# A linear-attention and SwiGLU kernel: batch 0 without arithmetic on GpSimd, a new order on VectorE and PE, and a weight load exchanged with a batch load

## The chip, the cores and the metric

The kernel runs on one core of a Trainium2 chip. The metric is the device time in microseconds (us), taken as the median of several executions. The record marks every execution told of here as fast, so that none has to be set aside. The profile's span is about 2 us shorter than the device time, because it starts with the first instruction. A time such as "at 21.2 us" counts from the start of that span. The engines are PE (TensorE, matrix products), VectorE (DVE in the profile), ScalarE (ACT), GpSimd (POOL) and SyncE (SP).

## The reference

```python
def _attn_ref(q, k, v):                  # 8 batches, 8 heads, 576 tokens, head size 64
    def phi(x):
        return np.where(x > 0, x, np.exp(x) - 1.0) + 1.0
    q_p, k_p = (phi(q), phi(k))
    kv = np.einsum('bhsd,bhse->bhde', k_p, v)
    z = np.sum(k_p, axis=2)
    num = np.einsum('bhsd,bhde->bhse', q_p, kv)
    den = np.einsum('bhsd,bhd->bhs', q_p, z)[..., None] + 1e-06
    return (num / den).astype(np.float32)

def _moe_ref(x, w_gate, w_val, w_out):   # 4608 tokens, 512 -> 1536 -> 512
    g = x @ w_gate
    silu = g * (1.0 / (1.0 + np.exp(-g)))
    return (silu * (x @ w_val) @ w_out).astype(np.float32)
```

The attention's output, with heads side by side, is the x of the feed-forward.

## The kernel before

The tokens are worked off in nine groups of 512. Each group passes through L1 (twelve blocks `fb` of the hidden size, gate and value) and then L2 (`wo`). These two stages keep PE full. Batches 0 and 1 are special. Batch 0 must pass through the whole attention before the first L1 matmul can start: this is the *prologue*. Batch 1 is worked off beside the first L1 and L2.

For batch 0 the feature map is built from two terms, since phi(x) = max(x, 0) + min(exp(x), 1). A head group `lp` (0 or 1) holds half of the heads. Before the change, GpSimd computed three of the instructions of lp 1:

```python
def k_max(lp):
    term(k16[0], kp[1], lp, 0.0, ALU.max, (nc.vector, nc.gpsimd)[lp])
def k_sum(lp):
    c = slice(P * lp, P * lp + P)
    (nc.vector, nc.gpsimd)[lp].tensor_tensor(out=kp[0][:, :, c], in0=kp[0][:, :, c], in1=kp[1][:, :, c], op=ALU.add)
def q_max(b, lp):
    term(q16[b], qp[1], lp, 0.0, ALU.max, (nc.vector, nc.gpsimd)[lp])
```

GpSimd also issues all loads, in program order. So its arithmetic stands between them:

```python
# ... loads of batch 0 and of w1's columns 0:256
q_max(0, 1)          # GpSimd
k_max(1)             # GpSimd
ld_w1(256, 512)
# ... VectorE, ScalarE and PE work of batch 0
k_sum(1)             # GpSimd
ld_w1(512, 768); ld_k(1); ld_w1(768, 1024); ld_w1(1024, 1280); ld_q(1); ld_w1(1280, 1536)
ld_w2(0); ld_v(1); ld_k(2); ld_w2(1); ld_w2(2)
```

`ld_w2(i)` loads a third of `wo`. In the first L2 stage, work of batches 1 and 2 is put into twelve slots, one after each four matmuls. The stage goes three times through the four output tiles (`i` = 0, 1, 2):

```python
w = at(12, [ # ... slots 0 to 2: transposes, z and k-v products of batch 1
    (2, lambda: exp_k(2, 0)), (2, lambda: exp_k(2, 1)), (3, lambda: den1(0)), (3, lambda: phi_k(2, 0)),
    (4, lambda: num1(0)), (5, lambda: den1(1)), (5, lambda: phi_k(2, 1)), (6, lambda: num1(1)),
    (7, lambda: den2()), (8, lambda: num2()), (9, lambda: exp_q(2, 0)), (10, lambda: exp_q(2, 1))])
# ...
for i in range(3):
    for t in range(4):
        l2(0, t, 4 * i, 4 * i + 4)
        for f in w[4 * i + t]:
            f()
        if i == 2:
            l2_out(0, t, V)      # VectorE copies the finished tile out of PSUM
vcast(2, 0)
```

`exp_k` runs on ScalarE and `phi_k` (one minimum, then two combined maximum-and-add instructions) on VectorE. `den1`, `den2` take PE, then ScalarE (ln, then exp); `num1`, `num2` take PE, then VectorE. The four output tiles lie in the PSUM banks (where PE puts its results) pV[0], pG[0], pV[1], pG[1]. The next L1 stage writes pG[0] and pV[0] first.

## Time and profile before

| what | before |
|---|---|
| device time, median of the four runs beside the changed kernel | 331.31 us (330.93 to 331.93) |
| first L1 matmul | 21.21 us |
| block 2 of L1 (the first one not mixed with the prologue) | 27.91 us |
| first L2 matmul | 45.53 us |
| second L1 stage begins | 61.76 us |
| from there to the end of the span | 267.6 us |

The table of stretches of the kernel before shows where PE has room. The columns are the stretch in us, its length, the busy time of each engine with its count of instructions, the granted PE clock (1.00 is full speed), the DMA share and GB/s.

```profile
8.00:16.00 8.00, 4.74 (x81) 3.51 (x78) 6.55 (x7) 5.81 (x7) 6.23 (x2) 1.00 1.19 185
16.00:20.00 4.00, 1.75 (x44) 1.07 (x44) 3.62 (x9) 1.17 (x2) 3.99 (x4) 0.83 0.74 91
20.00:28.00 8.00, 7.86 (x59) 3.35 (x60) 2.27 (x6) 2.24 (x6) 7.45 (x11) 0.66 1.10 146
28.00:44.00 16.00, 16.00 (x75) 7.27 (x75) 11.98 (x24) 15.22 (x17) 6.13 (x9) 1.00 1.33 200
```

From 28 us on PE is full at full clock, and only work that lets it start sooner can save time. Between 8 and 20 us PE is busy for about half of the time. Between 16 and 28 us the clock is also reduced. The trace's clock record gives 0.50 from 18.65 to 25.48 us.

The wait list of PE of the kernel before (who waited for whom: us in total, times, longest) names GpSimd three times:

```profile
PE pG_112 L393 <- POOL kp_72 L365: 1.3, 1, 1.3
PE pV_116 L165 <- POOL kp_71 L377: 1.3, 1, 1.3
...
PE pV_114 L405 <- POOL qp_74 L365: 1.0, 1, 1.0
```

Now the timeline of GpSimd and after it that of VectorE, before (start, duration, engine, line, operation, tiles, shape):

```profile
9.77 3.12 POOL L365 TENSOR_SCALAR qp_74<-q_0_65 128x1152 f16<-128x1152 f16 x1 [2.28 <-DMA q_0_65<-in_q_dram]
12.89 3.29 POOL L365 TENSOR_SCALAR kp_72<-k_0_63 128x1152 f16<-128x1152 f16 x1
...
17.69 2.39 POOL L377 TENSOR_TENSOR kp_71<-kp_71,kp_72 128x1152 f16<-128x1152 f16 x1
```

```profile
6.58 0.46 DVE L365 TENSOR_SCALAR kp_71<-ek 128x1152 f16<-128x1152 f16 x1 [0.74 <-ACT ek L362]
...
10.99 2.21 DVE L365 TENSOR_SCALAR qp_73<-eq 128x1152 f16<-128x1152 f16 x1
13.13 3.36 DVE L365 TENSOR_SCALAR kp_71<-ek 128x1152 f16<-128x1152 f16 x1
```

An instruction of the same form takes VectorE 0.46 us at 6.58 us, when GpSimd does no arithmetic. Beside GpSimd's instructions it takes 2.21 and 3.36 us. Each ends 0.31 us after GpSimd's instruction beside it: 13.20 after 12.89, and 16.49 after 16.18. In these two lines a busy VectorE is therefore mostly a blocked VectorE. The Trainium skill, "SBUF — State Buffer", section "Who interferes with whom", describes a port pair that the two engines share and that one of them holds for a whole instruction; these two pairs fit it.

The end of the first L2 stage, before: the first two output copies on VectorE, then PE's first matmul of the next stage.

```profile
60.13 0.68 DVE L306 TENSOR_SCALAR osb_102<-pV_114 128x512 f32<-128x512 f32 x1
60.73 0.68 DVE L306 TENSOR_SCALAR osb_103<-pG_112 128x512 f32<-128x512 f32 x1
```

```profile
61.76 0.38 PE L275 MATMUL pG_112<-xT_1_91,wg 128*128 128x512 f16 x1
```

The copy out of pG frees the bank at 61.4 us, and PE finishes L2 only then. Nothing waits.

### The profile page before, as it was taken

How to read it: one execution, taken by the hardware profiler on the slowest of the kernel's cores; microseconds unless marked ns; L12 is line 12 of the kernel's file. 1: busy time of each engine (PE TensorE's matmuls, PEld its weight loads, DVE VectorE, ACT ScalarE, POOL GpSimd, SP SyncE). 2: the span in 40 equal slices, each digit the busy share in tenths (PEclk: the TensorE clock that was granted, in tenths of full speed). 3: DMA queues.
4: the chain of work that ended last, by engine and by line, in shares of the span. 5: the costliest groups of instructions: out<-in, count | busy, mean ns of one | idle time of the engine just before them, and what ended most of it. 6: DMA issues, size and time to landing. Idle time of an engine off the chain costs nothing.

```text
span 329.4 us, 5083 instructions
## 1 busy us (share of the span) xinstructions
PE 317.2 (96%) x1957; PEld 150.0 (46%) x1957; DVE 220.0 (67%) x398; ACT 167.6 (51%) x239; POOL 40.5 (12%) x50
## 2 busy tenths in 40 slices
PE   8579999999999999999999999999999999999994
PEld 6434454454444444544444444444444444444443
DVE  3855776688978885888588858885887344234321
ACT  3626998927844684458445844584431233123310
POOL 7895410010001000100010000000000000000000
PEclk9969999999999999999999999999999999999999
DMA  7999999999395538363737340224112410140014
GB/s 106 175 125 177 203 207 208 218 225 152 65 159 105 105 80 166 57 115 75 148 71 125 63 100 15 26 54 97 27 24 48 98 32 0 31 91 8 2 32 96
DMA packets 40984, 32.18 MB, mean 98 GB/s; under 512 B 16256, under 2 KB 36480, under 8 KB 40960
## 3 DMA queue, kind: packets, MB, share of 16 engines
q0 software_dynamic: 20640, 18.88, 37.1%
q1 hardware_dynamic: 20160, 12.85, 17.8%
q8 instruction: 15, 0.25, 0.3%
q10 hardware_dynamic: 160, 0.13, 0.2%
q14 instruction: 9, 0.07, 0.1%
HBM read 37.75 MB, written 9.44 MB: 143 GB/s over the span
## 4 chain that ended last, share of the span: by engine, by line
PE 82%; ACT 5%; DVE 5%; issue 3%; DMA 2%; POOL 1%; SPq 0%; ACTq 0%; POOLq 0%; DVEq 0%
PE pG_112 L275 13%; PE pG_113 L275 12%; PE pV_114 L275 8%; PE pV_115 L275 8%; PE pV_116 L275 8%; PE pV_115 L296 7%; PE pG_112 L296 7%; PE pV_114 L296 7%; PE pG_113 L296 6%; DMA q_0_65<-in_q_dram 2%; PE pX_118 L165 2%; DVE hT_98 L281 1%; DVE kp_71 L365 1%; ACT ek L121 1%; ACT sil_100 L280 1%
## 5 line engine op out<-in xcount | busy, mean ns | idle before, releaser
L275 PEld LDWEIGHTS <-wv 128*128 128x128 f16 x432 | 42.5, 98 | 51.6 <-issue 1.1
L275 PEld LDWEIGHTS <-wg 128*128 128x128 f16 x432 | 41.4, 98 | 50.7 <-issue 2.1
L280 ACT ACTIVATE sil_100<-pG_112 128x512 f16<-128x512 f32 x51 | 30.5, 597 | 51.7 <-PE pG_112 L275 45.6
L280 ACT ACTIVATE sil_101<-pG_113 128x512 f16<-128x512 f32 x51 | 30.5, 597 | 37.8 <-PE pG_113 L275 35.1
L296 PEld LDWEIGHTS <-hT_98 128*128 128x128 f16 x228 | 21.4, 98 | 26.0 <-issue 1.5
L296 PEld LDWEIGHTS <-hT_99 128*128 128x128 f16 x192 | 18.4, 98 | 22.8 <-issue 0.9
L306 DVE TENSOR_SCALAR osb_104<-pV_115 128x512 f32<-128x512 f32 x9 | 6.2, 689 | 16.8 <-PE pV_115 L296 16.8
L215 DVE TENSOR_REDUCE den<-prod 128x12 f32<-128x768 f16 x18 | 17.0, 943 | 0.0
L296 PE MATMUL pV_114<-wo,hT_98 128*128 128x512 f16 x60 | 14.1, 379 | 0.2 <-DVE hT_98 L281 0.2
L296 PE MATMUL pV_115<-wo,hT_98 128*128 128x512 f16 x60 | 14.1, 379 | 0.0
L296 PE MATMUL pG_112<-wo,hT_98 128*128 128x512 f16 x60 | 14.1, 379 | 0.0
L281 DVE SCALAR_TENSOR_TENSOR hT_98<-pV_114,sil_100 128x512 f16<-128x512 f32 x11 | 7.6, 691 | 8.4 <-PE pV_114 L275 6.3
L304 ACT ACTIVATE osb_103<-pG_112 128x512 f32<-128x512 f32 x8 | 4.7, 584 | 16.3 <-PE pG_112 L296 16.3
L306 DVE TENSOR_SCALAR osb_105<-pG_113 128x512 f32<-128x512 f32 x8 | 5.5, 691 | 9.4 <-PE pG_113 L296 9.4
L296 PE MATMUL pG_113<-wo,hT_98 128*128 128x512 f16 x48 | 11.4, 380 | 0.0
L296 PE MATMUL pG_113<-wo,hT_99 128*128 128x512 f16 x48 | 11.1, 380 | 0.0
L296 PE MATMUL pV_114<-wo,hT_99 128*128 128x512 f16 x48 | 11.0, 379 | 0.0
L296 PE MATMUL pG_112<-wo,hT_99 128*128 128x512 f16 x48 | 11.0, 379 | 0.0
L296 PE MATMUL pV_115<-wo,hT_99 128*128 128x512 f16 x48 | 11.0, 379 | 0.0
L275 PE MATMUL pG_113<-xT_0_90,wg 128*128 128x512 f16 x27 | 10.5, 388 | 0.0
L275 PE MATMUL pG_113<-xT_0_92,wg 128*128 128x512 f16 x27 | 10.5, 388 | 0.0
L275 PE MATMUL pG_112<-xT_0_90,wg 128*128 128x512 f16 x27 | 10.5, 388 | 0.0
(240 smaller groups left out, 745.2 us busy)
## 6 DMA issues: line engine op xcount, KB each, us to landing
k_1_64<-in_k_dram POOLq DMA_DIRECT2D x4, 576.0 KB, 7.3
q_1_66<-in_q_dram POOLq DMA_DIRECT2D x4, 576.0 KB, 9.4
v_1_68<-in_v_dram POOLq DMA_DIRECT2D x4, 576.0 KB, 11.5
out_dram<-osb_102 SPq DMA_DIRECT2D x18, 128.0 KB, 2.4
out_dram<-osb_103 SPq DMA_DIRECT2D x18, 128.0 KB, 2.4
out_dram<-osb_104 SPq DMA_DIRECT2D x18, 128.0 KB, 2.4
out_dram<-osb_105 SPq DMA_DIRECT2D x16, 128.0 KB, 2.6
k_0_63<-in_k_dram POOLq DMA_DIRECT2D x3, 576.0 KB, 15.8
```

What stands on the lines that cost most here:

```text
L121: nc.scalar.activation(out=e[:, s, :], in_=src[b % 2][:, s, :], func=AF.Exp, bias=0.0, scale=1.0)
L165: nc.tensor.matmul(out=kvb[b][hh][:, 256 * lp:256 * lp + W], lhsT=kp[b % 2][rows, j, P * lp:P * lp + P], rhs=vv, start=(j == 0), stop=(j = ...
L215: nc.vector.tensor_reduce(out=den[:, HL * j0:HL * j1], in_=prod[:, 0:j1 - j0, :].rearrange("p j (l d) -> p (j l) d", d=D), axis=AX.X, op=A ...
L275: nc.tensor.matmul(out=ps[:, :], lhsT=src[:, i, P * fb:P * fb + P], rhs=xT[i][g % 2][:, :], start=(i == 0), stop=(i == 3))
L280: nc.scalar.activation(out=s[:, :], in_=pg[:, :], func=AF.Silu, bias=0.0, scale=1.0)
L281: nc.vector.scalar_tensor_tensor(out=hT[g % 2][:, fb, :], in0=pv[:, :], scalar=SC, in1=s[:, :], op0=ALU.mult, op1=ALU.mult)
L296: nc.tensor.matmul(out=pso[(g, t)][:, :], lhsT=hT[g % 2][:, fb, P * t:P * t + P], rhs=wo[:, fb, :], start=(fb == 0), stop=(fb == FB - 1))
L304: nc.scalar.activation(out=o[:, :], in_=ps[:, :], func=AF.Copy, bias=0.0, scale=1.0 / SC)
L306: nc.vector.tensor_scalar(out=o[:, :], in0=ps[:, :], scalar1=1.0 / SC, scalar2=None, op0=ALU.mult)
L365: eng.tensor_scalar(out=dst[:, :, P * lp:P * lp + P].rearrange("p j (s d) -> p s j d", d=D), in0=src[:, 2 * lp:2 * lp + 2, :].rearrange("p ...
```

## The change

The intent is to take GpSimd out of batch 0's arithmetic, so that VectorE is never blocked and loads are issued early. With that come a new order of instructions, and adjustments for a feed-forward that starts sooner: `wo`'s second third is loaded ahead of k of batch 2, and since that k now lands later, its `exp_k` and `phi_k` move to later slots. The lp-1 sum disappears: PE adds both terms instead. Cut to the core:

```diff
 def k_max(lp):
-    term(k16[0], kp[1], lp, 0.0, ALU.max, (nc.vector, nc.gpsimd)[lp])
+    term(k16[0], kp[1], lp, 0.0, ALU.max)
     # the same for q_max and k_sum
     # mm1(0, 1) takes both terms of k, as z0(0, 1) did already; ... cut
-    t0_copy(pV[0], 0, 0, 4, A)
-    t0_copy(pV[1], 0, 4, 8, V)
+    t0_copy(pV[0], 0, 0, 4, V)
+    t0_copy(pV[1], 0, 4, 8, A)
     # ... the order of the prologue on VectorE and PE: the terms with max are transposed first; cut
-    k_sum(1)
-    ld_w1(512, 768)
-    ld_k(1)
     # ... loads now after all other prologue work in program order, w1 256:512 and k(1) first; cut
     ld_v(1)
+    ld_w2(1)
     ld_k(2)
-    ld_w2(1)
     ld_w2(2)
@@ first()
-            (3, lambda: block(k16, ek, kp)), (7, lambda: block(q16, eq, qp)),
+            (3, lambda: block(k16, ek, kp)), (8, lambda: block(q16, eq, qp)),
-            (2, lambda: exp_k(2, 0)), (2, lambda: exp_k(2, 1)), (3, lambda: den1(0)), (3, lambda: phi_k(2, 0)),
-            (4, lambda: num1(0)), (5, lambda: den1(1)), (5, lambda: phi_k(2, 1)), (6, lambda: num1(1)),
-            (7, lambda: den2()), (8, lambda: num2()), (9, lambda: exp_q(2, 0)), (10, lambda: exp_q(2, 1))])
+            (3, lambda: den1(0)), (4, lambda: num1(0)), (5, lambda: den1(1)), (6, lambda: num1(1)),
+            (7, lambda: den2()), (7, lambda: exp_k(2, 0)), (7, lambda: exp_k(2, 1)), (8, lambda: num2()),
+            (8, lambda: phi_k(2, 0)), (9, lambda: phi_k(2, 1)), (10, lambda: exp_q(2, 0)), (11, lambda: exp_q(2, 1))])
```

More of the change, by code (lines that the diff above doesn't have):

```diff
@@ L152, with terms_k @@
     kvb = {}
+    def terms_k(b, lp):
+        return (kp[1], kp[0]) if (b, lp) == (0, 1) else (kp[b % 2],)
     def mm1(b, lp):
@@ L158, in mm1 @@
         for j in range(J):
-            for hh in range(2):
-                rows = slice(C * hh, C * hh + C)
-                if b < 2:
-                    vv = v16[b][rows, 2 * lp:2 * lp + 2, D * j:D * j + D]
-                else:
-                    vv = vm[b % 2][rows, j, :, :].rearrange("p l c -> p (l c)")[:, 130 * lp:130 * lp + W]
-                nc.tensor.matmul(
-                    out=kvb[b][hh][:, 256 * lp:256 * lp + W], lhsT=kp[b % 2][rows, j, P * lp:P * lp + P], rhs=vv,
-                    start=(j == 0), stop=(j == J - 1))
+            for (t, term_) in enumerate(terms_k(b, lp)):
+                for hh in range(2):
+                    rows = slice(C * hh, C * hh + C)
+                    if b < 2:
+                        vv = v16[b][rows, 2 * lp:2 * lp + 2, D * j:D * j + D]
+                    else:
+                        vv = vm[b % 2][rows, j, :, :].rearrange("p l c -> p (l c)")[:, 130 * lp:130 * lp + W]
+                    nc.tensor.matmul(
+                        out=kvb[b][hh][:, 256 * lp:256 * lp + W], lhsT=term_[rows, j, P * lp:P * lp + P], rhs=vv,
+                        start=(j == 0 and t == 0), stop=(j == J - 1 and t == len(terms_k(b, lp)) - 1))
     def zdiag(b, lp):
@@ L362, in exp0, with term @@
         nc.scalar.activation(out=e[:, 2 * lp:2 * lp + 2, :], in_=src[:, 2 * lp:2 * lp + 2, :], func=AF.Exp, bias=0.0, scale=1.0)
-    def term(src, dst, lp, val, op, eng=nc.vector):
-        eng.tensor_scalar(
+    def term(src, dst, lp, val, op):
+        nc.vector.tensor_scalar(
             out=dst[:, :, P * lp:P * lp + P].rearrange("p j (s d) -> p s j d", d=D),
@@ L376, in k_sum @@
         c = slice(P * lp, P * lp + P)
-        (nc.vector, nc.gpsimd)[lp].tensor_tensor(out=kp[0][:, :, c], in0=kp[0][:, :, c], in1=kp[1][:, :, c], op=ALU.add)
+        nc.vector.tensor_tensor(out=kp[0][:, :, c], in0=kp[0][:, :, c], in1=kp[1][:, :, c], op=ALU.add)
     def q_max(b, lp):
-        term(q16[b], qp[1], lp, 0.0, ALU.max, (nc.vector, nc.gpsimd)[lp])
+        term(q16[b], qp[1], lp, 0.0, ALU.max)
     def q_min(lp):
@@ L387, in z0 @@
     def z0(b, lp):
-        ts = (kp[1], kp[0]) if (b, lp) == (0, 1) else (kp[b],)
+        ts = terms_k(b, lp)
         for j in range(J):
@@ L400, in z0_copy, with t0 @@
                                     scalar2=None, op0=ALU.mult)
-    def t0(dst, lp, j0, j1):
-        for j in range(j0, j1):
-            for (src, first) in ((qp[1], True), (qp[0], False)):
-                nc.tensor.matmul(out=dst[:, P * (j - j0):P * (j - j0) + P], lhsT=src[:, j, P * lp:P * lp + P],
-                                 rhs=id16[:, :], start=first, stop=not first)
+    def t0(dst, lp, j0, j1, terms=(0, 1)):
+        for t in terms:
+            for j in range(j0, j1):
+                nc.tensor.matmul(out=dst[:, P * (j - j0):P * (j - j0) + P], lhsT=qp[1 - t][:, j, P * lp:P * lp + P],
+                                 rhs=id16[:, :], start=(t == 0 and j == j0), stop=(t == 1 and j == j1 - 1))
     def t0_copy(src, lp, j0, j1, eng):
@@ L440, in num0, with t0_all @@
             x0(nbank0[lp][i % 2][:, :], rr[:, i, :], xT[i][0][:, :])
+    def t0_all(lp, t):
+        for i in range(2):
+            t0(pV[i], lp, 4 * i, 4 * i + 4, (t,))
     warm(42, pX[1])
@@ L445 @@
     exp0(q16[0], eq, 1)
-    q_max(0, 1)
-    k_max(1)
-    ld_w1(256, 512)
     k_max(0)
@@ L452 @@
     q_max(0, 0)
-    q_min(0)
     z0(0, 0)
     z0_copy(0, 0)
-    warm(4, pX[1])
-    t0(pV[0], 0, 0, 4)
-    t0(pV[1], 0, 4, 8)
-    t0_copy(pV[0], 0, 0, 4, A)
-    t0_copy(pV[1], 0, 4, 8, V)
+    t0_all(0, 0)
+    warm(2, pX[1])
+    q_min(0)
+    q_max(0, 1)
+    t0_all(0, 1)
+    t0_copy(pV[0], 0, 0, 4, V)
+    t0_copy(pV[1], 0, 4, 8, A)
     exp0(k16[0], ek, 1)
-    warm(5, pX[1])
+    warm(7, pX[1])
     den0(0)
     q_min(1)
-    t0(pV[0], 1, 0, 4)
-    t0(pV[1], 1, 4, 8)
+    k_max(1)
+    t0_all(1, 0)
+    t0_all(1, 1)
+    t0_copy(pV[0], 1, 0, 4, V)
     k_min(1)
     mm1(0, 0)
+    r0_copies(0)
+    t0_copy(pV[1], 1, 4, 8, V)
     z0(0, 1)
-    t0_copy(pV[0], 1, 0, 4, V)
-    t0_copy(pV[1], 1, 4, 8, V)
-    r0_copies(0)
     z0_copy(0, 1)
-    k_sum(1)
-    ld_w1(512, 768)
-    ld_k(1)
-    ld_w1(768, 1024)
-    ld_w1(1024, 1280)
+    num0(0)
+    den0(1)
+    mm1(0, 1)
+    for c in (256, None, 512, 768, 1024):
+        if c is None:
+            ld_k(1)
+        else:
+            ld_w1(c, c + 256)
     ld_q(1)
@@ L482 @@
     ld_v(1)
+    ld_w2(1)
     ld_k(2)
-    ld_w2(1)
     ld_w2(2)
-    num0(0)
-    den0(1)
-    mm1(0, 1)
     def at(n, items):
```

## The prediction

> **What bounds it now.** From 21.2 us on PE never rests: the table of stretches gives PE 99 to 100% busy from 28 to 295 us at granted clock 1.00. So a gain can only come from starting the feed-forward sooner, or from the few places where PE still waits. The prologue is not PE-bound. The timeline shows GpSimd's two tensor_scalars taking 3.12 and 3.29 us (9.77 to 16.18) and, beside each, a VectorE minimum taking 2.21 and 3.36 us where its twin takes 0.46; each ends 0.31 us after GpSimd's does. That is what the Trainium skill, "SBUF — State Buffer", section "Who interferes with whom", says of a shared port held for a whole instruction, and this trace agrees. The chain of waits runs through both minima (2.13 and 3.29 us), then GpSimd's 2.40 us sum, then mm1 at 20.1 and the first feed-forward matmul at 21.2. The granted clock is also 0.50 from 18.7 to 25.5 us, after PE sat partly idle.
>
> **What changes.** GpSimd loses 8.8 us of arithmetic; VectorE gains one maximum and the q maximum (0.46 us each). The lp-1 sum goes (mm1 takes 18 more matmuls, about 0.5 us on PE). Stepping through the new order with these durations, I put the first feed-forward matmul near 16.5 us instead of 21.2. The gaps are short enough to keep the clock at 1.00, worth about 2 us more. Feed-forward block 2 would start near 21 instead of 27.9: about 6.8 us gained.
>
> **Does DMA allow it?** Before, a 256 KB weight half lands every 1.34 us and a 576 KB batch load every 2.84 us when queued. GpSimd now issues from 7.5 us on, not 16 to 21. Estimated landings from those rates: second half of w1's last columns near 36 against a need near 35.7, wo's first third 38.4 to 39 against 38.5. Just in time; I allow 0.3 us lost.
>
> **What is given back.** k of batch 2 is now exponentiated after den2, and phi_k(2) sits on VectorE in the last round of the first L2 stage, ahead of the output copies; the new instruction order confirms it. Before, those copies ran unhindered (60.1 to 62.6) and the next stage began at 61.8, 16.2 us after L2 began. Now, with L2's start as zero: den2 about 12, its ln and exp to 13.6, exp_k 14.7 and 15.8, phi_k 14.7 to 16.6, one copy, phi_k 17.2 to 19.1, and only then the copy that frees the bank which the next stage writes first: 19.8. Moving the q block from slot 7 to 8 adds 0.4 us at the transposes. So PE should stand idle about 3.5 us where it had no wait. The Trainium skill, "TensorE: Matmul & The Clock Gate", section "What's actually happening", says an idle window of about 3.4 us halves the clock; in this trace a half-busy stretch (15.2 to 18.6) sufficed. Chance of that here 60%, cost up to 1.7 us.
>
> Net: 6.8 - 0.3 - 3.9, then 0 to 1.7 lost: 1 to 3 us gained.
>
> **Prediction:** 329.2 us, 80% range 326.3 to 331.3. Chances: faster by over 2% 0.06, within 2% 0.93, slower 0.01.
>
> **What would show it.** No VectorE minimum over 0.8 us in the first 20 us; first feed-forward matmul at 16 to 17.5; clock 1.00 from 5 to 50 us; first L2 matmul at 38 to 39.5; a PE gap of 3 to 4 us near 55 to 59 ended by VectorE's copy out of pG; perhaps clock 0.50 after it; from there to the end 267.5 us as before.
>
> **What would make it wrong.** Weights landing later, so that PE waits on DMA in the first stage; a throttled prologue; or the wait at phi_k being shorter than I add up, which would give up to 324.5.

## The result, and the profile after

The changed kernel takes 329.76 us (329.70 to 330.44, four runs). The ratio to the kernel before is 0.9956, with a 95% interval of 0.9936 to 0.9976. A ratio here is the mean time of one kernel's fast runs over the mean of the other's fast runs of the same rounds, so it is not quite the ratio of the medians.

| what | before | after | gained so far |
|---|---|---|---|
| first L1 matmul | 21.21 | 16.79 | 4.4 us |
| block 2 of L1 | 27.91 | 21.50 | 6.4 us |
| first L2 matmul | 45.53 | 38.83 | 6.7 us |
| second L1 stage begins | 61.76 | 58.43 | 3.3 us |
| end of the span | 329.38 | 327.68 | 1.7 us |

The change gains 6.7 us up to L2. Then it gives 5.0 us back: 3.4 us by the end of that stage and 1.6 us after it. The same table of stretches, after:

```profile
8.00:16.00 8.00, 7.37 (x146) 5.45 (x145) 5.78 (x16) 6.40 (x8) 4.06 (x7) 1.00 1.28 195
16.00:20.00 4.00, 4.00 (x52) 2.03 (x46) 3.07 (x8) 2.10 (x3) 2.24 (x4) 1.00 1.36 200
20.00:28.00 8.00, 8.00 (x53) 3.56 (x52) 3.98 (x11) 7.12 (x11) 3.53 (x5) 1.00 1.41 198
...
44.00:60.00 16.00, 12.30 (x89) 4.64 (x83) 10.02 (x20) 12.25 (x15) 1.48 (x2) 0.95 1.21 208
60.00:62.00 2.00, 2.00 (x7) 0.70 (x6) 0.00 (x0) 1.67 (x2) 0.00 (x0) 0.56 1.18 257
```

PE is now almost full from 8 us on, at full clock, and DMA moves about 200 GB/s without a dip. The new loss is in the row from 44 to 60 us: 12.3 busy us of 16. The last row shows a reduced clock. VectorE's tensor_scalars of the prologue, after (this profile prints tiles without buffer numbers):

```profile
9.68 0.46 DVE L370 TENSOR_SCALAR qp<-eq 128x1152 f16<-128x1152 f16 x1
10.05 0.45 DVE L370 TENSOR_SCALAR qp<-q 128x1152 f16<-128x1152 f16 x1
...
11.23 0.45 DVE L370 TENSOR_SCALAR qp<-eq 128x1152 f16<-128x1152 f16 x1
11.60 0.45 DVE L370 TENSOR_SCALAR kp<-k 128x1152 f16<-128x1152 f16 x1
```

None of these is longer than 0.46 us. (The very first maximum, at 5.52 us, takes 0.69 us; why is not shown.) The wait list of PE has lost its GpSimd entries and has a new head:

```profile
PE pG L280 <- DVE osb L311: 3.7, 1, 3.7
```

The chain of waits of the changed kernel says what lies behind that copy (start, duration, what):

```profile
51.70 0.63 ACT r L430
52.33 1.06 ACT ek L121
...
53.42 0.47 DVE ek L125
...
53.91 1.43 DVE kp L127 x2
55.34 0.60 DVE osb L311
55.94 0.38 DVE ek L125
...
56.34 1.43 DVE kp L127 x2
57.77 0.61 DVE osb L311
...
58.43 1.86 PE pG L280 x4
```

PE ends L2 at 54.7 us. The bank pG[0] is freed by the second output copy (57.77). On VectorE that copy stands behind both `phi_k(2)` (L125 and L127, some 1.9 us each), and the first `phi_k` stands behind `exp_k` on ScalarE, which stands behind den2's exponential (L430). PE's timeline shows the consequence, and what follows it:

```profile
58.43 1.86 PE L280 MATMUL pG<-xT,wg 128*128 128x512 f16 x4 [3.70 <-DVE osb L311]
60.09 1.85 PE L280 MATMUL pV<-xT,wv 128*128 128x512 f16 x4
61.77 1.03 PE L280 MATMUL pG<-xT,wg 128*128 128x512 f16 x4
```

The same four matmuls show 1.86 and 1.85 us and later 1.03 us. The trace's clock record gives 0.50 from 58.33 to 61.74 us. The second stage to the end of the span takes 269.26 us against 267.62 before, 1.6 us more: half of 3.41 us at half clock would be 1.7.

### The profile page after: what moved, and what is told of

It reads as the page before. It is cut to its first block, busy times and chain, and to the rows that moved or that the text cites. A ratio compares the mean times of both kernels' runs of the same rounds, so it can differ in the third digit from the quotient of the medians.

```text
span 327.7 us, 5115 instructions
## 1 busy us (share of the span) xinstructions
PE 317.2 (97%) x1975; PEld 150.1 (46%) x1975; DVE 216.2 (66%) x400; ACT 167.8 (51%) x239; POOL 31.5 (10%) x47
## 4 chain that ended last, share of the span: by engine, by line
PE 90%; DVE 4%; DMA 3%; ACT 1%; issue 1%; POOL 1%; SPq 0%; POOLq 0%; DVEq 0%; ACTq 0%
PE pV L280 27%; PE pG L280 27%; PE pV L301 14%; PE pG L301 13%; PE pX L280 2%; DMA q<-in_q_dram 2%; PE pX L170 2%; PE pX L252 2%; DVE kp L127 1%; DVE qp L127 1%; DMA out_dram<-osb 1%; PE pX L200 1%; DVE osb L311 1%; DVE hT L286 0%; ACT eq L367 0%
## 5 line engine op out<-in xcount | busy, mean ns | idle before, releaser
L280 PE MATMUL pG<-xT,wg 128*128 128x512 f16 x408 | 105.9, 382 | 3.7 <-DVE osb L311 3.7
L280 PE MATMUL pV<-xT,wv 128*128 128x512 f16 x420 | 108.9, 381 | 0.0
L285 ACT ACTIVATE sil<-pG 128x512 f16<-128x512 f32 x102 | 60.6, 598 | 92.6 <-PE pG L280 83.7
L286 DVE SCALAR_TENSOR_TENSOR hT<-pV,sil 128x512 f16<-128x512 f32 x105 | 72.2, 690 | 52.6 <-PE pV L280 40.0
L301 PEld LDWEIGHTS <-hT 128*128 128x128 f16 x420 | 39.8, 98 | 48.4 <-issue 2.0
L301 PE MATMUL pV<-wo,hT 128*128 128x512 f16 x216 | 50.2, 379 | 0.0
L301 PE MATMUL pG<-wo,hT 128*128 128x512 f16 x204 | 47.6, 380 | 0.0
L127 DVE SCALAR_TENSOR_TENSOR kp<-k,ek 128x576 f16<-128x576 f16 x24 | 17.1, 755 | 0.4
L127 DVE SCALAR_TENSOR_TENSOR qp<-q,eq 128x576 f16<-128x576 f16 x24 | 17.1, 755 | 0.4
L233 DVE TENSOR_TENSOR qp<-qp,rden 128x768 f16<-128x768 f16 x18 | 17.1, 951 | 0.2
```

The lines of the kernel that those rows point to most:

```text
L127: nc.vector.scalar_tensor_tensor(out=dst[b % 2][:, :, D * l:D * l + D], in0=src[b % 2][:, l, :].rearrange("p (j d) -> p j d", d=D), scalar ...
L233: nc.vector.tensor_tensor(out=qv, in0=qv, in1=rden[:, HL * j0:HL * j1].unsqueeze(2).to_broadcast([P, HL * (j1 - j0), D]), op=ALU.mult)
L280: nc.tensor.matmul(out=ps[:, :], lhsT=src[:, i, P * fb:P * fb + P], rhs=xT[i][g % 2][:, :], start=(i == 0), stop=(i == 3))
L285: nc.scalar.activation(out=s[:, :], in_=pg[:, :], func=AF.Silu, bias=0.0, scale=1.0)
L286: nc.vector.scalar_tensor_tensor(out=hT[g % 2][:, fb, :], in0=pv[:, :], scalar=SC, in1=s[:, :], op0=ALU.mult, op1=ALU.mult)
L301: nc.tensor.matmul(out=pso[(g, t)][:, :], lhsT=hT[g % 2][:, fb, P * t:P * t + P], rhs=wo[:, fb, :], start=(fb == 0), stop=(fb == FB - 1))
```

## The experiments

The theory has three parts. First, GpSimd's arithmetic blocked VectorE; that made the prologue long. Second, the early issue of loads does not start L1 sooner, but it keeps weights ahead of PE. Third, the gain is given back because `phi_k(2)` stands ahead of the output copies on VectorE, and the idleness that follows halves PE's clock. The rivals were: a data dependence or the issue time of loads in the prologue; late data at the gap; and some other cause of the low clock. All kernels gave correct results. Positions on PE are from the trace of each run, and the times are medians.

### e1_copies_first: the output copies ahead of phi_k

```diff
-            (8, lambda: phi_k(2, 0)), (9, lambda: phi_k(2, 1)), (10, lambda: exp_q(2, 0)), (11, lambda: exp_q(2, 1))])
+            (10, lambda: exp_q(2, 0)), (11, lambda: exp_q(2, 1))])
@@ after the first L2 stage
+    phi_k(2, 0)
+    phi_k(2, 1)
     vcast(2, 0)
```

> The changed kernel with phi_k(2) moved on VectorE behind the four output copies of the first L2 stage. Theory (order on VectorE makes the 3.7 us gap and the gap makes the 3.41 us at half clock): the gap ended by the copy out of pG goes, the next stage starts near 54.7 instead of 58.3 us, the clock stays at 1.00; ScalarE's tail (exp_q, cast, table) then holds the third block about 1.4 us; net about 4 us off, near 325.8 us. Rival (the gap comes from k or v of batch 2 landing late): the gap stays, merely ended by another engine or DMA, and the time stays near 329.8.

Measured: 325.89 us, ratio 0.9851 (0.9829 to 0.9873). The next stage starts at 54.54 us, and no half-clock stretch follows. PE's wait list of this run:

```profile
PE pG L280 <- ACT sil L285: 1.4, 1, 1.4
```

So the place of the copies in VectorE's order was the cause of the gap, and late data was not. What is left is the wait for ScalarE that was expected. Its timeline shows the tail: the cast of v and the table load hold the first silu until 58.9 us.

```profile
56.43 1.17 ACT L147 ACTIVATE vm<-v 128x1152 f16<-128x1152 f16 x1
57.61 1.28 ACT L644 ACT_TABLE_LOAD   x1
58.91 0.60 ACT L285 ACTIVATE sil<-pG 128x512 f16<-128x512 f32 x1
```

### e2_fill_gap: the gap filled with matmuls that nobody reads

```diff
+    for _ in range(28):
+        nc.tensor.matmul(out=pX[1][:, 0:256], lhsT=ones[:, :], rhs=wo[:, 0, 0:256], start=True, stop=True)
     vcast(2, 0)
```

> The changed kernel with 28 matmuls that nobody reads (about 3.1 us) at the end of the first L2 stage, where PE stands idle. Theory (idleness halves the clock afterwards): the next stage still starts near 58.3, but no half-clock stretch follows, 1.7 us off, near 328.1. Rival (the half clock has another cause, such as the load on the chip): the stretch stays, time 329.8 or more.

Measured: 328.27 us, ratio 0.9922 (0.9901 to 0.9943). PE's timeline of this run:

```profile
54.71 3.22 PE L642 MATMUL pX<-wo,ones 128*128 128x256 f16 x28
58.57 1.02 PE L280 MATMUL pG<-xT,wg 128*128 128x512 f16 x4 [0.64 <-DVE osb L311]
```

The next stage starts as late as in the changed kernel, but its matmuls take 1.02 us and the clock stays at 1.00. From its start to the end of the span it takes 267.61 us, as in the kernel before. So the half clock comes from the idleness and costs 1.65 us (269.26 less 267.61). The rest of the 5.0 us is the gap of 3.7 us, less 0.3 us by which L2 itself was shorter than before. The Trainium skill, "TensorE: Matmul & The Clock Gate", section "What's actually happening", gives the window that decides on the clock as about 3.4 us. The stretch of 3.413 us agrees.

### e3_idle_gpsimd: GpSimd's work back, but for nobody

Two GpSimd instructions of the old form, in their old place, write to a buffer that is not yet in use.

```diff
+    def idle_work(src, i):
+        nc.gpsimd.tensor_scalar(
+            out=hT[1][:, 3 * i:3 * i + 3, :].rearrange("p f t -> p (f t)")[:, 0:J * P].rearrange("p (j s d) -> p s j d", s=2, d=D),
+            in0=src[:, 2:4, :].rearrange("p s (j d) -> p s j d", d=D), scalar1=0.0, scalar2=None, op0=ALU.max)
+    idle_work(q16[0], 0)
+    idle_work(k16[0], 1)
     warm(42, pX[1])
```

> The changed kernel with two GpSimd tensor_scalars of the old shape put back where they stood, written to a place nobody reads, so no data waits for them. Theory (VectorE is blocked while GpSimd's instruction runs): VectorE's tensor_scalars between 10 and 16 us stretch to 2 to 3.4 us each, ending about 0.3 us after GpSimd's; first feed-forward matmul at 20 to 23 instead of 16.8, block 2 later than 26; total 332 to 336. Rival (the old prologue was slow because lp-1 results came from GpSimd, i.e. data dependence, not contention): VectorE's durations stay near 0.46 and the first feed-forward matmul stays near 17; only the late DMA issue costs, as in the run with late issue.

Measured: 336.56 us, ratio 1.0164 (1.0129 to 1.0199); first L1 matmul at 21.63, block 2 at 26.34 us. GpSimd and then VectorE of this run:

```profile
9.67 3.15 POOL L452 TENSOR_SCALAR hT<-q 128x1152 f16<-128x1152 f16 x1 [2.13 <-DMA q<-in_q_dram]
12.81 3.28 POOL L452 TENSOR_SCALAR hT<-k 128x1152 f16<-128x1152 f16 x1
```

```profile
9.75 3.38 DVE L370 TENSOR_SCALAR qp<-q 128x1152 f16<-128x1152 f16 x1
13.05 0.67 DVE L419 CAST qT<-pV 128x512 f16<-128x512 f32 x1
13.65 2.77 DVE L370 TENSOR_SCALAR qp<-eq 128x1152 f16<-128x1152 f16 x1
16.33 0.44 DVE L370 TENSOR_SCALAR kp<-k 128x1152 f16<-128x1152 f16 x1
```

No data connects the two engines here, and VectorE's instructions stretch all the same, each to 0.3 us past GpSimd's end. The prologue is as late as before the change, so this contention alone is enough to make it so. In the kernel before, a dependence stood beside it: PE also waited for results of GpSimd (1.3, 1.3 and 1.0 us in its wait list). How much of the 4.4 us each of the two made there was not measured apart. The cast in between reads PSUM and runs in 0.67 us while GpSimd is in the middle of its second instruction: here only the instructions that read SBUF were blocked. With PE partly idle the clock is again reduced (0.50 from 13.4 to 20.2 us), but from the first L1 matmul to block 2 PE takes 4.71 us, as in the changed kernel. The kernel before took 6.70 us there, at half clock until 25.48 us, which is 4.27 us of it. The 2.0 us between these two times are about half of those 4.27, and they are the second part of the prologue's gain. The order of work on PE differs a little between the two. In e5 below, which keeps the old order and has full clock, this stretch takes 5.27 us with a wait of 0.4 us for a load in it.

### e4_late_issue: the loads held back

```diff
+    nc.gpsimd.tensor_scalar(out=hT[1][:, 0, 0:1], in0=rr[:, 2, 0:1], scalar1=0.0, scalar2=None, op0=ALU.max)
     for c in (256, None, 512, 768, 1024):
```

`rr` is ready at about 18 us, so all later loads wait for that.

> The changed kernel, GpSimd still without arithmetic but for one element, which holds back every load after w1's first columns until about 18 us, near where the kernel before issued them (16 to 21). Theory (the early start of the feed-forward comes from the port, and early issue only keeps the weights ahead of it): first feed-forward matmul stays near 16.8, but the loads land about 2 us later and PE waits for w1 1.5 to 2.5 us around 24 to 38; total 331 to 333. Rival (the gain in the prologue is the earlier issue): first feed-forward matmul moves to 20 or later.

Measured: 335.41 us, ratio 1.0138 (1.0110 to 1.0165). The first L1 matmul is at 16.28 us, so early issue does not start L1. But L2 starts at 44.09 us, 5.3 us later than in the changed kernel. PE's wait list:

```profile
PE pG L280 <- DVE osb L311: 3.6, 1, 3.6
PE pV L280 <- DMA wv<-in_moe_w_val_dram: 2.0, 3, 1.4
PE pG L280 <- DMA wg<-in_moe_w_gate_dram: 1.7, 1, 1.7
...
PE pX L280 <- DMA wg<-in_moe_w_gate_dram: 1.1, 1, 1.1
```

The expectation had 1.5 to 2.5 us of DMA waits; the run shows 4.8, and 335.4 us instead of 331 to 333. The restart explains the difference. The first load, issued at 17.93 onto a queue whose last load had landed at 16.95, lands at 22.38, and the next one of its size lands 2.42 us after it. In the changed kernel, where the queue never ran dry, these two land 1.31 and 1.34 us after the load before them. The second lands at 24.80 us instead of 19.55, and these 5.3 us are also the delay of L2. So early issue is not a side effect: without it 5.3 of the 6.7 us gained up to L2 are lost to waiting for weights.

### e5_before_no_gpsimd: the kernel before, with only the three instructions moved

```diff
 # k_max, q_max, k_sum: nc.vector in place of (nc.vector, nc.gpsimd)[lp]
-    q_max(0, 1)
-    k_max(1)
     ld_w1(256, 512)
     ...
+    q_max(0, 1)
     q_min(1)
+    k_max(1)
     t0(pV[0], 1, 0, 4)
```

> The kernel before with only its three GpSimd instructions (two maxima, one sum) put on VectorE beside their minima; VectorE's, PE's and the loads' order otherwise as before, so the loads are issued as soon as GpSimd gets to them. Theory (the port is the prologue's cost; the new order of PE and the missing sum are small): first feed-forward matmul at 17 to 18, clock 1.00 in the prologue, L2 near 39 to 40, no gap from phi_k; total about 326, faster than the whole change. Rival (the new order on VectorE and PE is what gains): first feed-forward matmul at 19 or later, total 328 or more.

Measured: 326.29 us, ratio 0.9848 (0.9821 to 0.9874); first L1 matmul at 16.64, L2 at 39.53, next stage at 56.79 us, full clock. This small part alone gains 5 us, three times what the whole change gains. It brings the early issue of loads too, since GpSimd has nothing else to do. It does pay one price that the change set out to avoid:

```profile
PE pV L296 <- DMA wo<-in_moe_w_out_dram: 1.5, 1, 1.5
```

### e6_old_slots and e7_old_slots_old_queue: the adjustments taken back one after the other

e6 is the changed kernel with the slots of `exp_k` and `phi_k` as they were before. e7 also puts `ld_k(2)` back ahead of `ld_w2(1)`.

```diff
 # e6 and e7
-            (7, lambda: den2()), (7, lambda: exp_k(2, 0)), (7, lambda: exp_k(2, 1)), (8, lambda: num2()),
-            (8, lambda: phi_k(2, 0)), (9, lambda: phi_k(2, 1)), ...
+            (2, lambda: exp_k(2, 0)), (2, lambda: exp_k(2, 1)), ..., (3, lambda: phi_k(2, 0)), ..., (5, lambda: phi_k(2, 1)), ...
 # e7 only
-    ld_w2(1)
     ld_k(2)
+    ld_w2(1)
```

> The changed kernel with exp_k and phi_k of batch 2 back in the slots they had before; the loads stay in the new order, so k of batch 2 lands near 47. Theory (the slots moved because k now lands too late for them): ScalarE stands waiting for k until 47 at the head of the chain of den1, and the chain ends some 3 us later; several PE gaps inside the first L2 stage instead of one at its end, next stage near 58.6; total 327.5 to 330, about the same as the change. If k landing does not matter: next stage near 55, total near 324.5.

Measured, e6: 328.25 us, ratio 0.9907 (0.9880 to 0.9935). ScalarE's timeline shows the wait for k at the head of den1's chain:

```profile
47.25 2.21 ACT L121 ACTIVATE ek<-k 128x1152 f16<-128x1152 f16 x2 [3.38 <-DMA k<-in_k_dram]
49.38 1.14 ACT L427 ACTIVATE rr<-pX,epst 128x448 f32<-128x448 f32 x2
```

PE then waits 2.3 us for ScalarE, the clock is halved once (from 52.4 to 55.8 us), and the next stage begins at 59.40 us, later than the 58.6 expected. So with the new loads the old slots do wait for k, as the change supposed. But the new slots are no better: 329.76 us (ratio 0.9956, 0.9936 to 0.9976) against 328.25 here.

> The same with the loads of k of batch 2 and of wo's second third also back in their old order: k lands near 44.4, wo's second third near 47 against a need near 45.7. Theory (the trade of the two loads and the move of the slots gave away more than the 1.3 us that it saved): one PE wait of about 1.3 us for wo, next stage near 56.4 at full clock; total near 326. Rival (the move was worth it): 328 or more.

Measured, e7: 325.93 us, ratio 0.9842 (0.9817 to 0.9867). PE waits 1.1 us for `wo`, and the next stage begins at 56.16 us at full clock. With new slots and new loads the changed kernel takes 329.76, with old slots and new loads 328.25, with both old 325.93. In the old slots, the exchange of the two loads costs 2.3 us, although it saves a wait of 1.1 us; the move of the slots, meant to fit the new loads, did not make this good and cost 1.5 us more. The fourth combination, new slots with the old loads, was not run. e5 and e7 differ in the rest of the change (the new order in the prologue, no sum of lp 1, batch 1's blocks and the order of its loads); their ratios, 0.9848 and 0.9842, are not told apart, so the runs do not show what that rest is worth.

### e8_copies_first_cast_later: e1, with the cast of v behind the first silu

```diff
-    vcast(2, 0)
     nc.scalar.preload_act_table_set("silu_and_others")
@@ the second L1 stage
-            sl[0] += [lambda: vcast(2, 1)]
+            sl[0] += [lambda: vcast(2, 0)]
+            sl[1] += [lambda: vcast(2, 1)]
```

> The changed kernel with the output copies ahead of phi_k, and besides the first half of v's cast behind the first silu of the next stage. In the run with only the copies moved, PE waited 1.4 us for ScalarE's silu. Theory (ScalarE's tail of exp, cast and table load is what is left): that wait falls to about 0.3 us, 324.8 us in all. Rival (VectorE, now late with phi_k, holds the next blocks instead): the wait moves to a matmul into pV, released by VectorE's hT, and the time stays near 325.9.

Measured: 325.89 us, ratio 0.9838 (0.9815 to 0.9860). This one is inconclusive. The wait shrinks from 1.4 to 0.33 us as expected, but a second one of 0.28 us for a later silu appears, and the time is not clearly under e1's. In the profiled execution the first loads landed late and block 2 began at 22.32 us instead of 21.48 in e1. Over the eight profiles that share the changed prologue, block 2 began between 21.30 and 22.32 us, so a difference of this size in one profile says nothing about the edit.

### e9_spread and e10_change_again: a version made from the findings, and a control

e9 keeps the prologue and the loads of the change. It puts `exp_k` into pauses of ScalarE after k has landed, the first `phi_k` into a pause of VectorE, and everything that may wait behind the output copies.

```diff
+            (3, lambda: den1(0)), (4, lambda: num1(0)), (4, lambda: exp_k(2, 0)), (5, lambda: den1(1)), (5, lambda: phi_k(2, 0)),
+            (6, lambda: num1(1)), (6, lambda: exp_k(2, 1)), (7, lambda: den2()), (8, lambda: num2_mm()),
+            (10, lambda: exp_q(2, 0)), (11, lambda: exp_q(2, 1))])
@@ after the first L2 stage; num2_mm is num2's part on PE, num2_x its part on VectorE
-    vcast(2, 0)
+    num2_x()
+    phi_k(2, 1)
@@ the casts of v as in e8
```

> A version built from what the runs showed: the changed kernel's prologue and order of loads, the output copies ahead of anything that may wait, exp_k of batch 2 in ScalarE's pauses after k lands (slots 4 and 6), the first phi_k in VectorE's pause, num2's products and the second phi_k behind the copies, v's cast behind the first silu. Theory: no PE wait over 0.5 us after the prologue, next stage at 54.7 to 55.3, clock 1.00 throughout, 324.6 us, some 1 us under the runs with only the copies moved. Rival: den1's and den2's chain, now behind exp_k, makes PE wait for num2 and the time stays at 325.9 or above.

Measured: 324.60 us, ratio 0.9808 (0.9786 to 0.9830). The clock is 1.00 up to the last matmul, and after the prologue PE's longest wait is 0.31 us. The next stage begins at 55.26 us, and 267.40 us follow. Its median is the lowest, 1.9% under the kernel before; whether it passes 2% is unclear by the interval.

> The changed kernel itself, unedited, on the same chip as a control: 329.8 us, a gap of 3.7 us before the second L1 stage and one half-clock stretch of 3.41 us after it, whatever the phase of the clock's windows.

Measured, the control: 330.47 us (329.69 to 331.12, six runs), ratio 0.9987 (0.9963 to 1.0011). PE's timeline:

```profile
58.69 1.09 PE L280 MATMUL pG<-xT,wg 128*128 128x512 f16 x4 [3.70 <-DVE osb L311]
59.58 1.91 PE L280 MATMUL pV<-xT,wv 128*128 128x512 f16 x4
```

The gap is again 3.70 us and the half-clock stretch again 3.413 us, here from 59.5 us on. One stretch is what the profiled execution shows. Its mean granted clock is 0.991. Three others of the six have 0.986 or 0.987 and take 330.83 to 331.12 us instead of 329.69 to 330.12, which by estimate is 3 us more at half clock. So a second such stretch is likely in these, but no trace shows it. The two measurements of the change, 0.9956 and 0.9987, together say that it gains something between nothing and half a per cent.

## Why the prediction was right

The forecast was 329.2 us within 326.3 to 331.3; the result is 329.76. Point by point:

- **The prologue.** Forecast: first L1 matmul near 16.5, block 2 near 21, a gain of 6.8 us. Measured: 16.79, 21.50, and 6.4 us. VectorE's minima all took 0.46 us, the clock stayed at 1.00, and e3 shows that the blocking by GpSimd alone makes a prologue as late as the old one.
- **DMA.** Forecast: loads just in time, 0.3 us lost. `wo`'s first third landed at 38.73 us and L2 began at 38.83; the profile lists no PE wait for DMA. The term of 0.3 us did not occur for the loads that it was meant for. But the other seven profiles with this prologue (e1, e2 and e6 to e10) list a wait of 0.3 to 0.6 us for w1's first columns, just after the first L1 matmul, which the forecast did not name. That the early issue carries the gain was only implied in the forecast; e4 shows it, and it weighs more than I had expected.
- **The 0.4 us at the transposes** for moving the q block to slot 8: wrong. PE did not wait there, because silu of block 10 ended at 39.64 us, just before PE asked for its bank. L2 took 15.9 us from first to last matmul, against 16.2 before. The forecast took PE to be 99 to 100% busy there before the change; the table of stretches has 15.66 of 16 us from 44 to 60 us.
- **The gap.** Forecast 3.5 us, ended by VectorE's copy out of pG; measured 3.70 us, and e1 removes it by the order alone.
- **The clock.** Forecast with a chance of 60% and up to 1.7 us; it came, in the control too, and e2 puts it at 1.65 us. Given as a chance, it entered the point estimate only in part: 6.8 - 0.3 - 3.9 is 2.6 us, and the estimate is 2.1 us under the kernel before, which leaves 0.5 us for the clock. That was 1.1 us too little. The 0.7 us of the two terms that did not occur made up for most of it, and this part of the close match is luck.

What the forecast did not ask is whether the change's parts all pull one way. They do not: the first part alone (e5) reaches 326.29 us.

## What to carry to other kernels

When a change moves an instruction that waits (for a load, or for another engine) to another place in an engine's order, look at what stands behind it there; here two output copies of 0.6 us became the reason for a 3.7 us gap on the bottleneck engine. The gap of 3.7 us cost 5.4 us here with the half clock after it, so count the aftermath of a gap too. And measure the parts of a combined change separately: here a small part held most of the gain, and the adjustments made around it took most of it back.

## What the Trainium skill lacked or had wrong

- "TensorE: Matmul & The Clock Gate", section "What's actually happening", gives the half clock as coming after at least one idle window of about 3.4 us. The stretches in the clock records here, apart from the last of each trace, are whole multiples of 3.413 us. With windows of that length counted back from their edges, the runs show it after windows in which PE worked: 1.59 of 3.41 busy us before (15.24 to 18.65), 1.86 of 3.41 in e6 (48.96 to 52.37), 0.82 of 3.41 in e10 (56.10 to 59.51). A window with 1.73 busy us in e4 (26.57 to 29.98) was not followed by it. So a partly idle window can be enough, and the busy time that the profile shows does not settle what the gate counts. Further down, the page tells of short pauses that lower the clock too, but no page says how idle a window must be. What the gate counts stays open.
- The same page and section give about 3.4 us of busy time for the return to full clock. The kernel before stayed at half clock for two windows (6.827 us); PE was busy for only 2.07 us of the first of them and for all of the second. This agrees, and is no lack.
- "SBUF — State Buffer", section "Who interferes with whom", says that the loser fully blocks, and it agrees. It lacks how soon a blocked VectorE instruction is done once GpSimd's has ended: 0.31 us in both pairs of the kernel before, less than the 0.46 us of the whole instruction alone (GpSimd's spans in this profile are rough).
- "DMA: Bandwidth & Descriptors", section "Anatomy of one DMA — SWDGE (gpsimd) path", gives a fit of 2.0 us plus bytes over 436 GB/s for one load issued by GpSimd. For 256 KB written that is an estimate of 2.6 us. The loads of w1 here, which also convert 512 KB of float32 to float16, took 3.87 us (before, issued at 16.13 us, while the load ahead of it landed only at 17.29) and 4.46 us (e4, on an empty queue) from issue to landing. With the 512 KB that are read, the estimate is 3.2 us, still less. The fit has no term for a conversion.
